# Reordering the hand-written schedule of a one-core infini-attention and MLP kernel: the same instructions, 234 and 235 changes of the matmul engine's tiling

## The chip, the cores and the metric

One core of a Trainium2 chip runs the kernel. The metric is the device time of one execution in microseconds (us). The engines are named as in the profile: PE is TensorE with its matmuls, PEld its weight loads, DVE is VectorE, ACT is ScalarE, POOL is GpSimd, SP is SyncE, whose queue (SPq) issues nearly all DMA transfers here.

## The reference, cut to what matters

The kernel adds an infini-attention and an MLP to its input x of 2048 tokens by 512 channels, in fp32:

```python
xn = _layernorm(x)
# attention: 32 heads of 16, 4 segments of 512 tokens; for each segment s
logits = einsum("bhqd,bhkd->bhqk", qs, ks) * scale + mask
p = softmax(logits);  a_dot = einsum("bhqk,bhkd->bhqd", p, vs)
pq = phi(qs);  a_mem = einsum("bhld,bhde->bhle", pq, M) / (einsum("bhld,bhd->bhl", pq, z)[..., None] + 1e-6)
o = g * a_mem + (1.0 - g) * a_dot
M = M + einsum("bhld,bhle->bhde", phi(ks), vs);  z = z + einsum("bhld->bhd", phi(ks))
# MLP: 512 -> 1792 -> 512
y = _layernorm(xn);  h = _gelu(y @ w1 + b1);  mlp = h @ w2 + b2
return x + o @ wo + mlp
```

## The kernel before

**Jobs and units.** The attention is cut into 16 units (4 segments by 4 groups of 8 heads), numbered 0 to 15. The work is a list of 1308 jobs, each a function that issues instructions to several engines. Jobs of one kind form streams (`streams()`), in which their order is fixed. `ORDER` is a string of 1308 letters: each letter names the stream whose next job is issued. `plan()` reads it, and the last loop of the kernel calls the jobs. The schedule is manual: every engine executes its own instructions in the order in which they were issued, and waits only for the semaphores of what it needs. So `ORDER` alone decides what stands behind what on PE, DVE, ACT, POOL and in SP's queue. `BANKS` gives, in the order of the calls, the PSUM bank (0 to 7) of each tile that `dense()` hands out.

**The jobs that matter here.**
- T(i,1), T(i,0) (`qk_proj`): keys and queries of unit i, 12 matmuls with 512 columns on the whole array (L495). ACT (L529) and DVE (L533) split the result into two fp16 halves, SP stores them to DRAM (L534 to L536) and loads them back in another layout into `kst` and `qst` (L542). For the memory, DVE forms phi in place (L544, L545).
- M(i,0) to M(i,11): row maxima of the logits. PE (L636) in two row halves of the array, DVE reduces (L643) into `mc`.
- R(i) (`m_row`): transposes `mc` (L514), splits the maxima (ACT L653, DVE L654), sends them through DRAM (SP L656, L659) into two more rows of `qst`. The scores S wait for it.
- S(i,t,n): logits minus maximum (PE L676 in row halves), exponential (ACT L681), triangle cut (POOL L690).
- pv and PV: probabilities times values (PE L705, in column tiles of 32); the second half is added by DVE (L718, L719).
- O(i,0) to O(i,2) (`o_norm`): normalises, adds the memory part and splits: DVE L729, ACT L555 and L556, DVE L560 and L561, POOL L735 and L737, ACT L740, POOL L741.
- Z, Qd, Q: the memory read (PE L586, ACT L591, DVE L592; Q: ACT L555 and L556, DVE L560 and L561, POOL L598).
- D(j,f): first MLP matmul, 12 matmuls with 256 columns on the whole array (L495 on `w1s`), DVE L771. G(j): gelu, with an ACT table load. H(j,c): split of the hidden values (POOL L785, ACT L786, POOL L787).
- e(j,n), n from 0 to 13: second MLP matmul, six matmuls in two row halves (L812). At n = 7 the halves exchange their PSUM banks, and `swap` makes PE wait until the earlier matmuls of that j have ended. DVE L818 adds the sum at n = 13.
- out(3,b): the output projection, 12 matmuls (L830), DVE L833 and the store L752. The four of the last segment end the program.
- X: loads and normalises 128 rows of x (SP L459).

PE thus works in three tilings: the whole array (T, D, V, out), two row halves (M, S, e, Qd and the transposes), and four column tiles (pv, PV, K).

Of the kernel before, what the change touches and what calls it, by code (L numbers as in the profile page):

```python
# [57 lines left out]
def streams():  # L58
# [43 lines left out]


ORDER = (
    "atacctcaetcttetcawvavcatwvcaxeacatxvdccwvxwfttyyyxbxyyuxgyyyzozoywouoxyccyzhoAzzAootAAppciiizAznpBiiABfBncAiBpi"
    "gzBszniipnzBiimchqqqiCBqBqiiioAoACBCCBCjjqiojqAjqjcioijoiCikskkBcmDskioBjiqiqCjjoijqCiqjsCqjDiftaoCCpgkkkpkjqCj"
    "oloojjljoloojiipkkkkiqihspqijqqipqijqiqjsjqqjaajfgpiiqkkkkmpliqqiooiqpDlqoDopohijjiojiijpolsjiqaqajqiqiqqiiqapk"
    "akmkktspaqijqiqjqiqajqbqajopijjgDfopkkkDkjjjlooooDlhjjjolqiqqiipkkkkjiqqijqqjjiqiqjjqiqiqiDkkkkmpliilfnplimpngr"
    "rmrjjponijqjqjinjipiskmkkmkaiijrijjoojiqsjqqjiqiiiqqkkkkihlqlfmlogojqjqjqqjjasoojmkkkkmqjiqjqjjaojjpipmooisikkk"
    "klpilhiofmgoooqiqpppqiqiqqqiiiqqpsosmoiqqiiqiqppsslooijqjojijojijoiaakkkkmpaijqjqjaqqqjiqqjiqjqiikmkkakbqiaqqah"  # L110
    "lolfqjjojqmjgjjoolmmkkkkmhjjoojjiitjiojiippkkkkliiilnfnimpligniinipmrrijjrsijqjqiqjiqjqiipkmkkksiqjqijqjqjiqjqi"
    "iqjqikmpkkkiprlqsphlfojmjgopjjlojpjoomokmkkkqiqisjojiqisjqiqijqqijqhiqqiiqjsqiiqppmkkkkilalofomqpgopaoooospmlaj"
    "qqqjqqjqjqiiqiqqqjqiqqipipooooiijooppoiaakkkkmajiqpisqqjiqjqjaiqaqhjqqqjqaaqmkkkkbjlfoljqjmjgojjqolmkkkkmmjjjoo"
    "jjioijoiiippkpkkkiinliifniiilnnimlgrpmjjrmjjjrrijikkpskkiqqijqiqijqqjiqjiqjqiqjiqiispqkpkskksqilqoplfojmjgjjjpo"
    "ooojolmkkkkiqjiqpsjiqiqijqjqiqijqjiqiqiqiiqqkksmkpikplolfjjqmjgjjjoooooklpkmkkjiiopjqiqijqjiqpjqiqijqiqqiqiiqik"
    "kpspkkqiplpoooopljjjqqqjqjjqooolkpskmkpkmqqqpqjpjqqqjqjqpqqjqjqqqkmkkkqlllqqqqqqqqqrrrr"
)

BANKS = (
    "050123614061756123401632157467410534702651305176254301741260523716405142730612547306651240651024615024612504612"
    "504650124650412650412650412650142650142650421607653420107642531076425031702531270531270531270132570132570132576"
    "135402761350427163054273106542736574326574326537425632754632574631072456310724563071245360712453620731620731067"
    "203617621073621073621073621037621037621037261702361475023671540263701524603175246031746013746013713460713471630"
    "471630463714067314056723410523674105236741052367410527410527410527410527410527140352671450326475103264751023674"
    "523674523647253647236547236475264735264107532410765324107265431067512043675120436751204736152047361520473615270"
    "346150312750317250317253107250371257013275027135027134650132754062751340621375460376054370567403056374065374065"
    "307645307645307642153076241076241076241076253410762534621075346210754316024310264310432610432610324610324612403"
    "246013752640163754207156437120564371205647312056473120564731206547321065473265104723607423460273460273642073642"  # L130
    "073642051736420157642031765420316750316705315631705630157630157630157306173504621357462017345620147536210436024"
    "136024316403216403216403216403216740536740536740536740536271406"
)


# [790 lines left out]
```

## Time and profile before

| | |
|---|---|
| device time, median of 3 | 691.06 us (690.85 to 691.38) |
| the profiled execution, device time | 691.51 us |
| span of its trace | 689.8 us |
| around the span | 1.7 us |
| mean granted TensorE clock | 0.999 of full speed |
| busy share PE / DVE / ACT / POOL | 99% / 79% / 73% / 49% |

The span runs from the first to the last instruction of the trace. A busy share is an average over the whole span. The rows below give the start of a group of like instructions, the time that it covers, and in brackets how long its engine was idle before it and what released it.

### The profile page before, as it was taken

To read this page: it belongs to the slowest core of one execution; us is meant where nothing else is said; L and a number is where in the kernel's file an instruction comes from. 1 tells how busy PE (TensorE), PEld (TensorE's weight loads), DVE (VectorE), ACT (ScalarE), POOL (GpSimd) and SP (SyncE) were. 2 spreads that over 40 slices of the span, in tenths; PEclk is the share of its full clock that TensorE was granted. 3 is DMA by queue.
4 is the path that set the end of the run, shared out by engine and by line. 5 is a ranking of instruction groups with operands and counts; after the bars stand their busy time and mean duration, and the time that the engine had idled before them with its cause. 6 is when DMAs were issued, how large, how long until landed. Compare 5 with 4: busy or idle time off the path is not lost.

```text
span 689.8 us, 17163 instructions
## 1 busy us (share of the span) xinstructions
PE 681.8 (99%) x6465; PEld 399.8 (58%) x6465; DVE 545.7 (79%) x1740; ACT 502.9 (73%) x972; POOL 340.5 (49%) x526
## 2 busy tenths in 40 slices
PE   8999999999999999999999999999999999999997
PEld 7855655565654546566554557567564456656653
DVE  6999968897795887998797787888688696969442
ACT  4486897788786659856794796766795687878870
POOL 5355567456535334663435355454353545446752
PEclk9999999999999999999999999999999999999999
DMA  9856342421203322421213224231120415140101
GB/s 277 249 149 201 92 109 49 117 55 31 65 24 102 94 67 45 122 50 33 69 26 98 58 73 100 72 86 32 41 72 24 132 19 154 17 109 2 19 1 62
DMA packets 51792, 55.15 MB, mean 80 GB/s; under 512 B 4782, under 2 KB 40636, under 8 KB 51708
## 3 DMA queue, kind: packets, MB, share of 16 engines
q1 hardware_dynamic: 49404, 49.84, 24.9%
q0 software_dynamic: 2304, 4.20, 3.8%
q8 instruction: 51, 0.84, 0.5%
q14 instruction: 33, 0.27, 0.1%
HBM read 36.99 MB, written 17.04 MB: 78 GB/s over the span
## 4 chain that ended last, share of the span: by engine, by line
PE 85%; DVE 5%; ACT 5%; DMA 2%; POOL 1%; issue 1%; SPq 0%; POOLq 0%; DVEq 0%; ACTq 0%
PE ps L495 36%; PE ps L812 17%; PE ps L705 10%; PE ps L830 6%; PE ps L676 5%; PE ps L636 5%; DVE ps L643 3%; ACT pt L681 2%; PE ps L586 2%; PE ps L514 1%; PE ps L843 1%; PE ps L321 1%; DMA wks<-in_A_wk_dram 1%; DMA qd<-hl 1%; PE ps L617 1%
## 5 line engine op out<-in xcount | busy, mean ns | idle before, releaser
L643 DVE CUSTOM_DVE_ANT_0 ps<-ps,mask 128x512 f32<-128x512 f32 (+3 forms) x512 | 233.9, 523 | 14.1 <-PE ps L636 12.9
L681 ACT ACTIVATE pt<-ps,qkcs 128x512 f32<-128x512 f32 (+1 forms) x384 | 206.8, 624 | 37.3 <-PE ps L676 35.2
L812 PE MATMUL ps<-w2s,hT 64*128 64x512 f16 x1344 | 176.6, 375 | 0.1
L495 PE MATMUL ps<-xnT,w1s 128*128 128x256 f16 x1344 | 158.0, 273 | 0.0
L690 POOL TENSOR_SCALAR_AFFINE_SELECT pt<-pt 128x256 f32<-128x256 f32 x256 | 101.0, 421 | 98.2 <-ACT pt L681 97.2
L495 PEld LDWEIGHTS <-w1s 128*128 128x128 f16 x1344 | 127.2, 98 | 28.5 <-issue 11.6
L787 POOL TENSOR_TENSOR hT<-hh,hT 128x512 f16<-128x512 f32 x64 | 67.7, 1057 | 86.3 <-ACT hT L786 82.7
L812 PEld LDWEIGHTS <-hT 64*128 64x128 f16 x1344 | 76.3, 94 | 49.8 <-issue 5.9
L705 PE MATMUL ps<-pt,vt 128*32 128x512 f32 (+3 forms) x1024 | 77.1, 435 | 0.1
L771 DVE SCALAR_TENSOR_TENSOR hT<-ps,sc,sr 128x256 f32<-128x256 f32 x112 | 52.4, 478 | 26.9 <-PE ps L495 26.7
L643 DVE DVE_READ_ACCUMULATOR2_ANT mc<- 128x1 f32 x512 | 71.0, 139 | 0.0
L636 PE MATMUL ps<-kst,qst 48*128 48x256 f16 (+3 forms) x512 | 66.7, 297 | 1.1 <-DMA qst<-qd 0.3
L676 PE MATMUL ps<-qst,kst 50*128 50x512 f16 (+3 forms) x512 | 66.2, 297 | 0.0
L786 ACT ACTIVATE hT<-hh 128x512 f16<-128x512 f32 x64 | 36.6, 572 | 33.3 <-POOL hh L785 32.9
L705 PEld LDWEIGHTS ps<-pt,vt 128*32 128x32 f32 x1024 | 30.5, 109 | 43.0 <-issue 32.4
L785 POOL TENSOR_SCALAR hh<-hT,sc 128x512 f32<-128x512 f32 x64 | 42.2, 660 | 25.7 <-ACT hT L778 24.1
L735 POOL TENSOR_TENSOR nN<-nN,oT 128x512 f32<-128x512 f32 x16 | 20.3, 1269 | 61.1 <-DVE oT L561 61.1
L778 ACT ACTIVATE hT<-hT,b1t 128x256 f32<-128x256 f32 x112 | 46.5, 495 | 0.2
L495 PE MATMUL ps<-xnT,wqs 128*128 128x512 f16 x192 | 44.2, 380 | 0.0
L495 PE MATMUL ps<-xnT,wks 128*128 128x512 f16 x192 | 44.1, 379 | 0.0
L495 PE MATMUL ps<-wvs,xnT 128*128 128x512 f16 x192 | 44.0, 379 | 0.0
L830 PE MATMUL ps<-wos,oT 128*128 128x512 f16 x192 | 43.3, 379 | 0.6 <-POOL oT L741 0.6
(225 smaller groups left out, 883.1 us busy)
## 6 DMA issues: line engine op xcount, KB each, us to landing
kd<-hl SPq DMA_DIRECT2D x48, 128.0 KB
qd<-hl SPq DMA_DIRECT2D x48, 128.0 KB
kst<-kd SPq DMA_DIRECT2D x32, 192.0 KB
qst<-qd SPq DMA_DIRECT2D x32, 192.0 KB
acc<-in_A_x_dram SPq DMA_DIRECT2D x16, 256.0 KB
acc<-in_B_b_dram POOLq DMA_DIRECT2D x16, 256.0 KB, 4.2
out_dram<-acc SPq DMA_DIRECT2D x16, 256.0 KB
xt<-in_A_x_dram SPq DMA_DIRECT2D x14, 256.0 KB
```

The lines of the kernel that those rows point to most:

```text
L495: T.matmul(p, wsl(ws, k, a), xsl(xs, k, b), start=s0 and i == 0, stop=s1 and i == 3 * n - 1)
L636: T.matmul(p[:, o:o + n], stk[i, 0][r, t, P * qb:P * qb + P], stk[i, 1][r, t, :n], start=True, stop=True)
L643: V.tensor_tensor_reduce(p[:, o:o + n], p[:, o:o + n], mask[:, 512 - n:], 1.0, -3e38, OP.add, OP.max, mc[:, 16 * b + 4 * t + qb:16 * b + 4 ...
L676: T.matmul(p[:, o:o + n], stk[i, 1][r, t, P * kb:P * kb + P], stk[i, 0][r, t, P * kb:], start=True, stop=True)
L681: A.activation(e[:, OFF[kbs[0]]:OFF[kbs[0]] + o], p[:, :o], AF.Exp, scale=qkcs[:, 1, i % NG:i % NG + 1])
L690: G.affine_select(v, v, pattern=[[0, 2], [1, P]], compare_op=OP.is_ge, fill=0.0, base=0, channel_multiplier=-1)
L705: T.matmul(p[32 * c:32 * c + 32, P * kb:], vt[s, kb][:, 4 * g + c, 16 * odd:16 * odd + 32], pt[i, 2 * c + odd][:, OFF[kb]:OFF[kb] + LEN[kb ...
L771: V.scalar_tensor_tensor(hz[:, fi, :], p[:, :256], col(F1 + fh), srow[hs][:, own], op0=OP.mult, op1=OP.mult)
L778: A.activation(z, z, AF.Gelu_apprx_tanh, bias=b1t[:, FH * (j % 2) + f:FH * (j % 2) + f + 1])
L787: G.tensor_tensor(hT[:, z, 1, :], t, hT[:, z, 0, :], op=OP.subtract)
L812: w = T.matmul(pes[j][a], hTs[fh][r, fi, u, P * a:P * a + P], w2s[r, fo, v, :], start=n == 0 and m == 0, stop=fi == FH - 1 and m == 2, ski ...
L830: T.matmul(p, o[:, u, P * b:P * b + P], wos[:, g, v, :], start=i == 0, stop=i == 3 * NG - 1)
```

## The change

Only the two tables `ORDER` and `BANKS` are replaced. The first 60 jobs are the same, and behind them the same jobs come in another order. Both kernels issue 1308 jobs and the same instructions (9859 rows on PE in each). PE changes between its three tilings 234 times in the order before and 235 times in the new one. The banks are handed out anew for the new order. The last line of `ORDER` shows the kind of change; all other lines behind the first half line differ in the same way.

```diff
 ORDER = (
...
-    "kpspkkqiplpoooopljjjqqqjqjjqooolkpskmkpkmqqqpqjpjqqqjqjqpqqjqjqqqkmkkkqlllqqqqqqqqqrrrr"
+    "iqikkkkoiplooopljjjqojqmjqqjolospkkkpkqmpqjpqqqqqqjqqjjqpqjqjmqqqkkkkqlqqqqlqqqlqqqrrrr"
 )
...
 BANKS = (
...
-    "136024316403216403216403216403216740536740536740536740536271406"
+    "714302743102743102740342317024317021473050763205376207356204207"
 )
```

In these lines k is a pv or PV job, q an e job, j an S job, l an O job, o a D job, m a memory job, p a G or H job, i an M or R job and r an out job.

SP's queue behind T(2,1) and T(2,0), the keys and queries of unit 2, before: the stores to `kd_93` and `qd_95` are theirs, L542 loads them back, and L459 loads rows of x for the next segment.

```order
L656 DMA md_98<-mhl 32x2x128
L659 DMA qst_90<-md_98 2x2048 x2
L534 DMA kd_93<-hl 8x16x512
L535 DMA kd_93<-hl 8x16x512
L536 DMA kd_93<-hl 8x16x512
L459 DMA xt<-in_A_x_dram 128x512 x2
L534 DMA qd_95<-hl 8x16x512
L535 DMA qd_95<-hl 8x16x512
L536 DMA qd_95<-hl 8x16x512
L542 DMA kst_91<-kd_93 48x4x512 x2
L542 DMA qst_89<-qd_95 48x4x512 x2
L791 DMA acc<-in_A_x_dram 128x512
```

The same place now:

```order
L534 DMA kd_93<-hl 8x16x512
L535 DMA kd_93<-hl 8x16x512
L536 DMA kd_93<-hl 8x16x512
L656 DMA md_98<-mhl 32x2x128
L659 DMA qst_90<-md_98 2x2048 x2
L534 DMA qd_95<-hl 8x16x512
L535 DMA qd_95<-hl 8x16x512
L536 DMA qd_95<-hl 8x16x512
L542 DMA kst_91<-kd_93 48x4x512 x2
L542 DMA qst_89<-qd_95 48x4x512 x2
L791 DMA acc<-in_A_x_dram 128x512
L459 DMA xt<-in_A_x_dram 128x512 x2
```

The x loads have moved from ahead of the query stores to behind the loads into `kst` and `qst`, and the trip of unit 1's maxima (L656, L659) from ahead of the key stores to behind them.

DVE around R(15), the maxima of the last unit, before: L718 and L719 belong to PV(14,1), L654 to R(15), L729 to O(14,0), L771 to the D(15) jobs.

```order
L718 SCALAR_TENSOR_TENSOR nN<-ps_9812,bg,nN 128x512
L719 SCALAR_TENSOR_TENSOR nD<-ps_9812,eo,nD 128x512
L654 SCALAR_TENSOR_TENSOR mhl<-ps_9851,mhl 32x64
L654 SCALAR_TENSOR_TENSOR mhl<-ps_9852,mhl 32x64
L729 STREAM_SHUFFLE oT<-nD 128x512
L771 SCALAR_TENSOR_TENSOR hT_116<-ps_9875,sc,sr 128x256
```

The same place now:

```order
L718 SCALAR_TENSOR_TENSOR nN<-ps_9829,bg,nN 128x512
L719 SCALAR_TENSOR_TENSOR nD<-ps_9829,eo,nD 128x512
L771 SCALAR_TENSOR_TENSOR hT_116<-ps_9848,sc,sr 128x256
L654 SCALAR_TENSOR_TENSOR mhl<-ps_9863,mhl 32x64
L654 SCALAR_TENSOR_TENSOR mhl<-ps_9864,mhl 32x64
L729 STREAM_SHUFFLE oT<-nD 128x512
```

D(15,0) has moved from behind R(15) to ahead of it, so that three D jobs instead of four are left between R(15) and the first scores S(15,0,0) that wait for it.

PE where e(14,6) ends and e(14,7) begins, before: `ps_9979` and `ps_9980` are the two sums of e(14), and the pair comes in the other order from e(14,7) on; L676 is S(15,1,0) and then S(15,1,1).

```order
L812 MATMUL ps_9979<-w2s,hT_115 128x512
L812 LDWEIGHTS hT_115
L812 MATMUL ps_9980<-w2s,hT_115 128x512
L676 LDWEIGHTS kst_92
L676 MATMUL ps_10148<-qst_90,kst_92 128x512
...
L676 MATMUL ps_10159<-qst_90,kst_92 128x128
L812 LDWEIGHTS hT_115
L812 MATMUL ps_9980<-w2s,hT_115 128x512
```

The same place now, with the sums `ps_10016` and `ps_10017`:

```order
L812 MATMUL ps_10016<-w2s,hT_115 128x512
L812 LDWEIGHTS hT_115
L812 MATMUL ps_10017<-w2s,hT_115 128x512
L812 LDWEIGHTS hT_115
L812 MATMUL ps_10017<-w2s,hT_115 128x512
```

The two score jobs that stood between the last matmul of e(14,6) and the first of e(14,7) have moved away, so that nothing is left between them.

At the end of the program, between PV(15,1) and out(3,0), there are 11 e jobs now and 10 before; between PV(14,1) and pv(15,0,0) 4 and 6; between PV(15,0) and pv(15,1,0) 15 and 16. There the order of the instructions on DVE, ACT and POOL is the same in both.

## Rows read from the trace of the kernel before

**Rows 1.** The page: busy time (share, instructions) of each engine; chain that ended last, by engine.

```profile
PE 681.8 (99%) x6465; PEld 399.8 (58%) x6465; DVE 545.7 (79%) x1740; ACT 502.9 (73%) x972; POOL 340.5 (49%) x526
PE 85%; DVE 5%; ACT 5%; DMA 2%; POOL 1%; issue 1%; SPq 0%; POOLq 0%; DVEq 0%; ACTq 0%
```

**Rows 2.** Timeline of PE at 300 us: start, length, instruction, count.

```profile
300.00 2.79 PE L495 MATMUL ps<-xnT,w1s 128*128 128x256 f16 x24
302.73 0.39 PE L636 MATMUL ps<-kst,qst 48*128 48x512 f16 x2
```

**Rows 3.** Windows: from:to, sum, busy of PE, PEld, DVE, ACT, POOL, clock, DMA, GB/s.

```profile
35.00:80.00 45.00, 44.25 (x411) 25.87 (x412) 43.35 (x161) 34.74 (x71) 24.43 (x33) 1.00 0.53 161
585.00:602.00 17.00, 16.81 (x187) 10.63 (x180) 16.84 (x73) 12.75 (x27) 7.51 (x14) 1.00 0.13 22
```

**Rows 4.** Timeline from T(2,0) to M(2,0): SP's queue and PE.

```profile
97.06 0.89 SPq L459 DMA_DIRECT2D xt<-in_A_x_dram  x2
...
104.66 0.79 SPq L542 DMA_DIRECT2D qst<-qd  x2
...
108.98 0.33 PEld L636 LDWEIGHTS <-qst 48*128 48x128 f16 x5 [0.36 <-DMA qst<-qd]
```

**Rows 5.** Timeline ahead of T(8,0).

```profile
332.61 1.26 POOL L737 TENSOR_TENSOR nN<-nN,ame 128x512 f32<-128x512 f32 x1
332.66 1.50 DVE L544 TENSOR_SCALAR phk<-phk,qksc 128x512 f32<-128x512 f32 x1
...
334.94 0.18 PEld L586 LDWEIGHTS ps<-phq,zr 64*128 64x128 f32 x1 [0.64 <-DVE phk L545]
```

**Rows 6.** All instructions of L544: count, shortest/median/longest in ns, first and last start.

```profile
L544 DVE TENSOR_SCALAR phk<-phk,qksc x12: 466/996/1503, 20.6 to 445.3; 128x512 f32<-128x512 f32 x12
L544 DVE TENSOR_SCALAR phq<-phq,qksc x12: 474/478/1396, 168.9 to 612.8; 128x512 f32<-128x512 f32 x12
```

**Rows 7.** Timeline from R(14) (601.14) to S(14,0,0) (605.69) and T(15,0) (608.19).

```profile
601.14 0.12 PEld L514 LDWEIGHTS ps<-ident,mc 64*96 64x96 f32 x2 [0.44 <-DVE mc L643]
...
601.33 0.43 PE L705 MATMUL ps<-pt,vt 128*32 128x128 f32 x8
...
605.69 0.61 PE L676 MATMUL ps<-qst,kst 50*128 50x512 f16 x6
...
607.65 0.61 PE L676 MATMUL ps<-qst,kst 50*128 50x256 f16 x2
...
608.19 0.60 PE L495 MATMUL ps<-xnT,wqs 128*128 128x512 f16 x2
```

**Rows 8.** Timeline from R(15) to S(15,0,0) (641.54), and S(15,2,0) (644.31).

```profile
636.01 0.25 PE L514 MATMUL ps<-ident,mc 64*96 64x64 f32 x2
...
636.20 5.41 PE L495 MATMUL ps<-xnT,w1s 128*128 128x256 f16 x48
...
641.54 0.91 PE L676 MATMUL ps<-qst,kst 50*128 50x512 f16 x8
...
644.31 0.65 PE L676 MATMUL ps<-qst,kst 50*128 50x512 f16 x2
```

**Rows 9.** Timeline of the last 25 us, from pv(15,1) to out(3,0).

```profile
665.01 0.15 PEld L705 LDWEIGHTS ps<-pt,vt 128*32 128x32 f32 x6 [0.42 <-POOL pt L690]
...
667.60 0.69 DVE L561 SCALAR_TENSOR_TENSOR rc<-rc,rt 128x512 f32<-128x512 f32 x1
...
667.73 6.89 PE L812 MATMUL ps<-w2s,hT 64*128 64x512 f16 x60
668.26 0.75 DVE L718 SCALAR_TENSOR_TENSOR nN<-ps,bg,nN 128x512 f32<-128x512 f32 x1
...
669.91 4.21 PEld L812 LDWEIGHTS <-hT 64*128 64x128 f16 x42 [0.56 <-PE ps L812]
...
674.55 2.67 PE L830 MATMUL ps<-wos,oT 128*128 128x512 f16 x11
...
677.85 8.16 PE L830 MATMUL ps<-wos,oT 128*128 128x512 f16 x37 [0.63 <-POOL oT L741]
```

More of the change, by code (lines that the diff above doesn't have):

```diff
@@ L104 @@
 ORDER = (
[L105 to L114, printed above, removed]
@@ L115 @@
-    "ooojolmkkkkiqjiqpsjiqiqijqjqiqijqjiqiqiqiiqqkksmkpikplolfjjqmjgjjjoooooklpkmkkjiiopjqiqijqjiqpjqiqijqiqqiqiiqik"
-    "kpspkkqiplpoooopljjjqqqjqjjqooolkpskmkpkmqqqpqjpjqqqjqjqpqqjqjqqqkmkkkqlllqqqqqqqqqrrrr"
+    "atacctcaetcttetcawvavcatwvcaxeacatxvdccwvxwfttyyyxbxyyuxgyyyzzuwyooooyzAoyAxzoozpiphizcntAcAccizipczBizfzBAniBi"
+    "BpgBCACniipiBnqiiqCqmhAqAiBiqBioBCCoBjAjojqiqjisqAsjqjisooiiCckmkBDBisikkoCjqijojiqjcCqiCqjjftiCCpogkkkkCjqpjlo"
+    "oojjljoloojipiskkkkihqapiqiqjipsqqjiqqjijqqijaqijfgomkiDqpapiqqqhiskkkpDlooiojlijoDojjiiopjiqaqaqipsjqiqlipitap"
@@ new lines @@
+    "kakkmkqqjqaiqqqjiqaqabiqjjopjjigpfokkkkjjloojjljpoooqjliqihkkkkiqiDqjiqjqmqjiqiDqqjqjjqiaqqikkkkDpliiinDlnflimp"
+    "grnjjsmjrrojsiijnjiikkskmkpijioripjjojiqqjqiiqjqipqikkkkhmiqlolfmjgojqqjqjjaqjlookkkmkmjiqjqqjjoijojmpiikkkapks"
+    "lhiopoolfimipgopopqiqqqqiqipqiimqqooiiqlqipioojiqjqjqjsiopojiiojasamakkpkmkijqqjqjaqsjqqqjiqiqjiakkisbkkhqiaqal"
+    "olfojqjqqjmjgjjoolkkkmkmjhjmoojjitijjoiiikpkkkpnliiilfniimgniiplniprrpjjirijqjqqjiiqqjiksmakkkmiqjqijsqjqijqiqj"
+    "qijpriikkkkhqiplqomlfmjjgopjolojjjookkkmkmiiqjqqppqiiojiqjsqiqjiqmjqhjpqiqqispikkkkliqqipoolsfoimpgooopmojjqqqa"
@@ L117 @@
+    "qjqqjqisjpqaiqqiipqiqiooqpiqljipooosooaaikkkkiqsqjaiqpqiqjjqqajaqijqqjqqaakkmmkkbjlolhjfjqmjgqjjolokmkkkmjjoojm"
+    "jijooiijkkkpiipinpkliiilfnlniiinmigrrpmjjjrjjrjsiikkkksiqiqjiqqpijqqjiqjiqqjjmqiqipqiikkkkqiplqolfjmjsgopoljmjo"
+    "ojmjoposkkkkiqjpsiqjiqiqjsiqqjiqiqjiqqijqiqiikskpkpkilolfqjjqmjgjpjjooookklmkkoijipojqijqijqpjiqqjiiqqpiqpqipqi"
+    "iqikkkkoiplooopljjjqojqmjqqjolospkkkpkqmpqjpqqqqqqjqqjjqpqjqjmqqqkkkkqlqqqqlqqqlqqqrrrr"
 )
 BANKS = (
-    "050123614061756123401632157467410534702651305176254301741260523716405142730612547306651240651024615024612504612"
@@ L123 @@
[L123 to L131, printed above, removed]
-    "136024316403216403216403216403216740536740536740536740536271406"
+    "050123614061756123401632157467032471456024371560247532610472653014657230614230576410576410574067156047156047516"
@@ new lines @@
+    "041075641075610765410761450764510741064571064571542603762154307462513407265406725620475276045276074256077406746"
+    "312056734014725630147253601427534127534127543125741325741325714352160741351264031752640317640253140245310425310"
+    "423103542103541270561342740651302174653242610754324610753624107562413507624135067241367241376234127613423761432"
+    "761432673142673142567017342056017345675426103746251403754103751401753403157043157043162745031672540364157023642"
+    "531642513642135643145623164152315642376012341520746351402765314632051764235042173652410736205364103271503624713"
@@ new lines @@
+    "205647132647132647312467312467312471632471632174637213406572061435720635147026351745021457021452704175204175204"
+    "175240137054236052130764521430521435021345042135042342714560327016453725643754623756243755624357624573624574362"
+    "750143762503174625753014267503124753012465174623051274360754123716057042316045723410623416023416023416023041623"
+    "104165302174265301472635021576432016423061402361423062143062143061243061234064057123403605637124305671320471320"
+    "714302743102743102740342317024317021473050763205376207356204207"
```

## The prediction, put on record before the run

> **What bounds the kernel now.** I read the page first: PE is busy for 99% of the span, and the chain that ended last lies on PE for 85% [rows 1]. No other engine is near that over the whole span. So the time is PE's own work plus what PE loses between instructions, and an order can change only the second part: the cost of changing the tiling, waits, and the end. I then followed PE along its timeline and noted each place where it, or its weight loads, stood still for another engine or a transfer. The windows say which engine is behind: from 35 to 80 us DVE works 43.35 of 45 us, and from 585 to 602 us 16.84 of 17 us, at full clock in both [rows 3]. Everywhere else DVE, ACT and POOL have slack, and only single late results reach PE.
>
> The sum is made against the profiled execution, 691.51 us, of which 689.8 are span. It lies 0.45 above the median of 691.06, so I subtract 0.45 at the end. The bound of what can be told from no change is 0.2%, here 1.4 us.
>
> **Changes of tiling: +0.1.** The pitch shows their price. Two D jobs take 302.73 - 300.00 = 2.73 us up to the next instruction in row halves [rows 2]; four D jobs, again with a change behind them, take 641.54 - 636.20 = 5.34 [rows 8]. The difference of 2.61 is two D jobs, so a D is 1.305 and one change about 0.1. 234 changes are some 23 us, and 235 are 0.1 more. An e is 0.65: 42 of its matmuls take 674.55 - 669.91 = 4.64 us with a change behind them [rows 9], 0.108 each, and it has six.
>
> **The head, 35 to 80 us: -0.3.** Every job of the weight scaling, the first T, M and D comes in a new order there, but DVE has the same work. Only its idle 45 - 43.35 = 1.65 us can be gained [rows 3], and PE can be held longer if DVE's results come in a worse order. I take -0.3, with -1.0 (most of the idle time) and +0.7 (as much again as less than half of it) as bounds.
>
> **T(2,0) to M(2,0): -0.3.** M(2,0) waits 0.36 for `qst` [rows 4]. Its stores stood in SP's queue behind the x loads at 97.06, whose issue took 0.89, and the load L542 came at 104.66. Now the x loads stand behind. PE has the same six D, six S and one e to do in between. Bounds: 0 (ACT's half comes late in any case) and -0.36. What moves behind, the x loads, is wanted only by the next segment.
>
> **T(8,0): -0.5.** DVE's L544 took 1.50 us at 332.66, beside POOL's L737, which had begun 0.05 earlier and ran to 333.87 [rows 5]. A free L544 takes 0.47 [rows 6]. Behind it L545 came late, and the weights of Qd(7) waited 0.64 for DVE [rows 5]. Between T(8,1) and Qd(7) PE now has three e instead of two beside the same D and three S, 0.65 more to do, which covers it. Bounds 0 and -0.64.
>
> The Trainium skill bears on this, page "SBUF — State Buffer", section "Who interferes with whom": an operation of DVE in a two-port mode, which tensor_scalar can enter, and one of POOL take a shared port pair in turn, and the loser blocks until the other's whole instruction has ended. The trace agrees: 1.50 is nearly the 1.21 that L737 still had to run plus the free 0.47. By the row alone the term stands at -0.5; by the rule the gain can be lost again wherever the new order puts another L544 behind a POOL operation, which is the second rival.
>
> **M(14) and R(14): +0.4 and +0.2.** From 585 to 602 us DVE is full with the row maxima of M(14), and R(14) already waits 0.44 for `mc` [rows 3, 7]. The order before gives PE 13 e jobs between M(14,0) and R(14); the new one gives it 12 and PV(13,1), which is 0.43 at most [rows 7] against 0.65. PE has less to do in the same DVE time: 0.2 to 0.4 more waiting; bounds 0 and +0.7. Behind R(14) on DVE, L718 and L719 of PV(13,1) now stand ahead of L654 where L575 stood: two operations of 0.75 each [rows 9] for four small ones of some 0.2, so the maxima leave about 0.7 later. The trip from R to S was 605.69 - 601.14 = 4.55 without a wait [rows 7]; PE now has a D (1.3), T(15,1) (two D in columns, 2.6), an e (0.65) and changes, about 4.8. Some 0.2 may be waited for S(14,0,0), between 0 and 0.7.
>
> **T(15,0): -0.3.** S(14,0,2) at 607.65 and T(15,0) at 608.19 are 0.54 apart [rows 7], where a pair of S (0.108 a matmul at most, as in e) and a change need some 0.3. ACT is late with T(15,1) behind it. e(12,12) now stands between T(15,1) and S(14,0,0), which gives ACT 0.65 more. Bounds 0 and -0.3.
>
> **R(15) to S(15,0,0): +0.5.** Here PE had four D behind R, and S came 641.54 - 636.01 = 5.53 us after R without a wait [rows 8]. Now three D stand there, 4.0 to 4.2 us. The trip of the maxima through DRAM needs what the other units show: at most 4.55 in unit 14 [rows 7], at most 5.53 here. If it needs 4.3 PE waits 0.2; if it needs 5.0, 0.9. I take 0.5. SP and DVE have nothing new in the trip; L771 of D(15,0) goes ahead of L654, but its matmuls end before R's.
>
> **S(15,2,0): -0.2.** The pair of S(15,2,0) took 0.65 [rows 8] where a pair of that form takes 0.39 [rows 2]; its two banks are given free by ACT and by DVE's L818. With other banks that wait of 0.26 goes, or another comes: -0.26 to +0.3.
>
> **Swap: +0.2.** e(15,7) begins behind e(15,6) with nothing in between, and its weights wait 0.56 for PE to run empty [rows 9]. The 18 matmuls ahead of it end at 667.73 + 18 x 0.108 = 669.67, and the next begin at 669.91, so the emptying costs 0.24. In the order before this happens once in the tail; S(15,1,0) and S(15,1,1) hide it for e(14,7). In the new order nothing stands there: once more, 0 to +0.24.
>
> **The tail: -1.4.** This is the largest term. Before, pv(15,1) waits for POOL's triangle cut, 0.42 at first [rows 9]. L718 then cannot start when PV(15,1) is done, because DVE is at Q(15)'s L560 and L561 until 668.29; it starts at 668.26. From there the chain of O(15) (DVE, ACT, DVE, POOL, ACT, POOL) is serial and ends some 9.5 us later, when out(3,0), whose twelfth matmul needs it, goes on at 677.85. PE has done ten e and 11 matmuls of out(3,0) by 674.55 + 11 x 0.217 = 676.94 (512 columns cost twice a D matmul's 1.305 / 12) and waits 0.91 (0.63 at the matmul, the rest in its weight load). In the new order 11 e stand behind PV(15,1): 0.65 of the 0.91 is covered. PV(15,1) itself comes later against DVE and POOL, since 16 instead of 15 e stand ahead of pv(15,1,0) and Q(15) has been issued three e earlier: the 0.4 of the cut goes, and so does the 0.5 that L718 was held. Together 0.91 + 0.45, all of the waiting. At worst only 0.65 and part of the cut go, -0.9; at best -1.6. The work that PE does there is only shifted, and the last 37 matmuls and the store behind them stay as they are.
>
> **The sum.** 0.1 - 0.3 - 0.3 - 0.5 + 0.4 + 0.2 - 0.3 + 0.5 - 0.2 + 0.2 - 1.4 = -1.6, so 689.9 for the profiled execution, less 0.45: 689.4.
>
> **Rivals.**
> - The tail is gained and the rest gives it back: R(14), M(14) and R(15) at their upper bounds (0.7 + 0.7 + 0.9 in place of 1.1) and no gain in the head and at T(8,0) (0.8). That is -1.6 + 1.2 + 0.8 = +0.4, 691.5; with half of it, 690.5. For it speaks that distances behind most R are shorter now; against it that PE had slack in those trips.
> - Slower: L544 meets POOL elsewhere. There are 24 of them, 466 to 1503 ns, half of those on keys at 996 or more [rows 6], each up to 1.03 late, and PE pays for one of them now. It decides where PE's next need follows at once, at Qd or T. At four more paid in full, and the gain at T(8,0) gone, -1.6 + 4.1 + 0.5 = +3.0: 694.1; from three on it is 693.1, slower by more than can be told from no change. Against it: most late L544 cost PE nothing in the order before.
> - More than I take: the head gives its whole idle time and T(2,0), T(8,0) and the tail their bounds, while M(14) and R(15) cost nothing: -1.6 - 0.7 - 0.2 - 0.2 - 1.1 = -3.8, 687.3.
> - Nothing happens: other waits appear at the tail, for example Q(15) ahead of the last S on ACT, and the order is worth 0.1: 691.1.
>
> **How the numbers follow.** My sum holds with 0.45 (688.5 to 690.2), the give-back with 0.25, more than I take with 0.12, nothing with 0.08, slower with 0.10. Faster by over 0.2%, below 689.7: two thirds of the first and all of the third, with a little of the second, 0.46; slower 0.11; the rest 0.43. The range goes from 687.6 to 691.6: it leaves out the far end of the third and the slower cases. The likeliest case's own range is 688.5 to 690.2.
>
> **What would show it.** In the new profile: PE's busy time within 0.5 us of 681.8; no [POOL] release at pv(15,1) and out(3,0) going on without a wait behind O(15); no wait for `qst` ahead of M(2,0); S(15,0,0) with a wait for a transfer behind three D; the pair e(14,6), e(14,7) with a weight load that waits for PE; DVE as full as before from 35 to 80 us. The prediction is wrong if out(3,0) still waits for POOL, if new releases by DVE or DMA at Qd, T or S sum to over 1.5 us, or if the head moves by more than 1 us.

## The result, and the profile after

The new order is slower. Its median over 6 runs is 694.43 us (693.08 to 695.44), against 691.10 us (690.44 to 691.52) for the order before in 6 runs beside it: a ratio of 1.0043, 95% interval 1.0031 to 1.0055, so 2.1 to 3.8 us longer. The forecast was 689.4 us with a range to 691.6. The profiled execution took 694.2 us, of which 692.5 are span; the clock was full in both.

The page of the new order, with the two lines that answer to [rows 1]:

```profile
PE 681.8 (98%) x6465; PEld 392.6 (57%) x6465; DVE 542.2 (78%) x1740; ACT 504.3 (73%) x972; POOL 341.6 (49%) x526
PE 80%; DVE 10%; DMA 5%; ACT 2%; issue 2%; SPq 0%; POOL 0%; DVEq 0%; POOLq 0%; ACTq 0%
```

PE's busy time is the same to a tenth, so the 2.7 us of span are all time between PE's instructions. The shares of DVE and DMA in the chain that ended last have doubled or more. To find the places I took, for sets of jobs that both orders have issued in full, the start of the next job on PE:

| jobs done | next job | before | after | after - before |
|---|---|---|---|---|
| 365 | T(4,1) | 166.88 | 165.90 | -0.98 |
| 539 | a D job | 266.91 | 265.97 | -0.94 |
| 659 | an e job, now a transpose | 323.90 | 324.22 | +0.32 |
| 731 | R(8) | 373.62 | 372.54 | -1.08 |
| 933 | K, now M | 479.17 | 480.20 | +1.03 |
| 993 | S(11,1,0) | 508.27 | 509.56 | +1.29 |
| 1086 | pv(12,1,1) | 563.64 | 565.29 | +1.65 |
| 1241 | e(13,12), now D(15,4) | 642.19 | 646.22 | +4.03 |
| | out(3,0) | 674.55 | 677.93 | +3.38 |
| | end of the span | 689.8 | 692.5 | +2.7 |

The new order leads by a microsecond at 166 and at 373 us. It loses 1.3 from 266 to 322 us, 2.1 from 373 to 479 us and 2.4 from 564 to 646 us. The list of PE's waits names a transfer for the largest (line waited at, what was waited for: us in total, times, longest):

```profile
PE ps L676 <- DMA qst<-md: 2.1, 2, 1.6
PE ps L636 <- DMA qst<-qd: 0.7, 1, 0.7
PE ps L514 <- DVE mc L643: 0.7, 2, 0.5
```

The 1.6 is at R(15). The timeline there, which answers to [rows 8]:

```profile
638.82 0.26 PE L514 MATMUL ps<-ident,mc 64*96 64x64 f32 x2
639.01 4.10 PE L495 MATMUL ps<-xnT,w1s 128*128 128x256 f16 x36
...
639.93 0.30 SPq L656 DMA_DIRECT2D md<-mhl  x1
...
643.07 0.54 SPq L659 DMA_DIRECT2D qst<-md  x2
...
644.75 0.73 PE L676 MATMUL ps<-qst,kst 50*128 50x512 f16 x6 [1.64 <-DMA qst<-md]
```

The maxima go to DRAM with L656 and come back with L659, which SP issues when the store has landed. From L656 to L659, here called the trip, it took 643.07 - 639.93 = 3.14 us. In the trace before it took 1.39 to 1.49 in ten of the 16 trips and 1.77 to 2.66 in the other six, 2.02 at R(15); now it takes 1.39 to 1.45 in nine and 2.31 to 3.18 in seven. R(15) before:

```profile
637.49 0.30 SPq L656 DMA_DIRECT2D md<-mhl  x1
...
639.51 0.53 SPq L659 DMA_DIRECT2D qst<-md  x2
```

In the new order the three D jobs behind R(15) last 4.10 us; R to S took 5.93. The DMA view from 639.9 to 643.1 us (queue: packets, MB, share of 16 engines' time) shows what else was under way:

```profile
q1 hardware_dynamic: 80, 0.02, 2.6%
q8 instruction: 1, 0.02, 2.4%
```

q1 carries the store, 80 packets; q8 is of the kind instruction, so what it moves is code, and one 16 KB piece of it is moved here, from 640.79 to 642.03. Where nothing else moves, the packets of the store pass in 0.2 us. Here the windows from 640.7 to 641 us (first two lines) and from 642 to 642.2 us (last line) show 75 of them beside the piece and the last five only when it has passed:

```profile
q8 instruction: 1, 0.02, 25.9%
q1 hardware_dynamic: 75, 0.02, 23.0%
q1 hardware_dynamic: 5, 0.00, 6.9%
```

The last packet ends at 642.17, and L659 follows 0.90 us later. Before, a piece of code (637.51 to 638.47) met the store of R(15) too, at the cost of 0.6 us that the four D jobs covered.

The second place is M(11,0), which waits for its queries:

```profile
448.21 0.33 SPq L656 DMA_DIRECT2D md<-mhl  x1
451.21 0.56 SPq L659 DMA_DIRECT2D qst<-md  x2
451.87 0.58 SPq L534 DMA_DIRECT2D qd<-hl  x1
...
456.79 0.79 SPq L542 DMA_DIRECT2D qst<-qd  x2
...
461.12 0.39 PE L636 MATMUL ps<-kst,qst 48*128 48x512 f16 x1 [0.72 <-DMA qst<-qd]
```

Here R(10)'s trip stands in SP's queue ahead of the query stores of T(11,0), and it too lasted 3.00 us (451.21 - 448.21), with a piece of code in it (449.15 to 450.10). In the order before those stores began at 449.16 and L542 came at 454.16, 2.6 earlier.

The third stretch shows no large wait, but a full DVE; in the timeline single waits for it, and the window from 290 to 300 us (columns as in [rows 3]):

```profile
283.99 2.78 PE L495 MATMUL ps<-xnT,w1s 128*128 128x256 f16 x24 [0.23 <-DVE phk L545]
298.97 2.78 PE L495 MATMUL ps<-xnT,w1s 128*128 128x256 f16 x24 [0.16 <-DVE mc L643]
301.91 0.39 PE L676 MATMUL ps<-qst,kst 50*128 50x512 f16 x2 [0.16 <-DVE mc L643]
290.00:300.00 10.00, 9.84 (x94) 6.33 (x91) 9.96 (x42) 4.81 (x10) 3.86 (x4) 1.00 0.41 89
```

Before, PE worked all of these 10 us and DVE 9.53. The waits of PE for DVE from 266 to 322 us, with one of 0.20 at 272.45, sum to 0.75; there were none before.

What answers to [rows 4] to [rows 7], at T(2,0), ahead of T(8,0) and at R(14):

```profile
102.90 0.79 SPq L542 DMA_DIRECT2D qst<-qd  x2
104.23 0.90 SPq L459 DMA_DIRECT2D xt<-in_A_x_dram  x2
108.01 0.43 PEld L636 LDWEIGHTS <-qst 48*128 48x128 f16 x6
...
332.40 0.48 DVE L544 TENSOR_SCALAR phk<-phk,qksc 128x512 f32<-128x512 f32 x1
332.57 1.44 POOL L737 TENSOR_TENSOR nN<-nN,ame 128x512 f32<-128x512 f32 x1
334.19 0.30 PEld L586 LDWEIGHTS ps<-phq,zr 64*128 64x128 f32 x4
...
602.57 0.26 PE L514 MATMUL ps<-ident,mc 64*96 64x64 f32 x2 [0.49 <-DVE mc L643]
```

M(2,0) and Qd(7) no longer wait, as forecast; R(14) still does, and longer: its weight load stood for 0.76 where it stood for 0.44 before. In the tail, which answers to [rows 9], POOL's two waits are still there, 0.42 at pv(15,1) and 0.52 at out(3,0), and e(14,7) now waits 0.56 for PE to run empty:

```profile
660.45 0.98 PEld L812 LDWEIGHTS <-hT 64*128 64x128 f16 x12 [0.56 <-PE ps L812]
668.04 0.28 PEld L705 LDWEIGHTS ps<-pt,vt 128*32 128x32 f32 x8 [0.42 <-POOL pt L690]
670.46 7.54 PE L812 MATMUL ps<-w2s,hT 64*128 64x512 f16 x66
677.93 10.74 PE L830 MATMUL ps<-wos,oT 128*128 128x512 f16 x48
680.50 7.67 PEld L830 LDWEIGHTS <-oT 128*128 128x128 f16 x37 [0.52 <-POOL oT L741]
```

### The profile page after: what moved, and what is told of

Its sections match the earlier page's. It is cut to its first block, busy times and chain, and to the rows that moved or that the text cites. A ratio compares the mean times of both kernels' runs of the same rounds, so it can differ in the third digit from the quotient of the medians.

```text
span 692.5 us, 17151 instructions
## 1 busy us (share of the span) xinstructions
PE 681.8 (98%) x6465; PEld 392.6 (57%) x6465; DVE 542.2 (78%) x1740; ACT 504.3 (73%) x972; POOL 341.6 (49%) x526
## 4 chain that ended last, share of the span: by engine, by line
PE 80%; DVE 10%; DMA 5%; ACT 2%; issue 2%; SPq 0%; POOL 0%; DVEq 0%; POOLq 0%; ACTq 0%
PE ps L495 34%; PE ps L812 17%; PE ps L705 9%; PE ps L830 5%; PE ps L676 5%; DVE ps L643 5%; PE ps L636 4%; DMA qd<-hl 2%; PE ps L586 1%; DMA qst<-qd 1%; DVE mc L643 1%; PE ps L514 1%; DMA md<-mhl 1%; ACT pt L681 1%; PE ps L321 1%
## 5 line engine op out<-in xcount | busy, mean ns | idle before, releaser
L681 ACT ACTIVATE pt<-ps,qkcs 128x512 f32<-128x512 f32 (+1 forms) x384 | 207.3, 620 | 43.2 <-PE ps L676 41.7
L812 PE MATMUL ps<-w2s,hT 64*128 64x512 f16 x1344 | 174.1, 376 | 0.1
L690 POOL TENSOR_SCALAR_AFFINE_SELECT pt<-pt 128x256 f32<-128x256 f32 x256 | 102.6, 427 | 94.6 <-ACT pt L681 93.9
L812 PEld LDWEIGHTS <-hT 64*128 64x128 f16 x1344 | 70.0, 94 | 56.6 <-issue 4.2
L771 DVE SCALAR_TENSOR_TENSOR hT<-ps,sc,sr 128x256 f32<-128x256 f32 x112 | 51.6, 477 | 24.1 <-PE ps L495 22.1
L676 PE MATMUL ps<-qst,kst 50*128 50x512 f16 (+3 forms) x512 | 64.7, 298 | 2.2 <-DMA qst<-md 2.1
L705 PEld LDWEIGHTS ps<-pt,vt 128*32 128x32 f32 x1024 | 31.9, 109 | 40.2 <-issue 30.3
L676 PEld LDWEIGHTS <-kst 50*128 50x128 f16 x512 | 26.2, 94 | 31.7 <-issue 12.1
```

Of the source, the lines that this page charges most:

```text
L676: T.matmul(p[:, o:o + n], stk[i, 1][r, t, P * kb:P * kb + P], stk[i, 0][r, t, P * kb:], start=True, stop=True)
L681: A.activation(e[:, OFF[kbs[0]]:OFF[kbs[0]] + o], p[:, :o], AF.Exp, scale=qkcs[:, 1, i % NG:i % NG + 1])
L690: G.affine_select(v, v, pattern=[[0, 2], [1, P]], compare_op=OP.is_ge, fill=0.0, base=0, channel_multiplier=-1)
L705: T.matmul(p[32 * c:32 * c + 32, P * kb:], vt[s, kb][:, 4 * g + c, 16 * odd:16 * odd + 32], pt[i, 2 * c + odd][:, OFF[kb]:OFF[kb] + LEN[kb ...
L771: V.scalar_tensor_tensor(hz[:, fi, :], p[:, :256], col(F1 + fh), srow[hs][:, own], op0=OP.mult, op1=OP.mult)
L812: w = T.matmul(pes[j][a], hTs[fh][r, fi, u, P * a:P * a + P], w2s[r, fo, v, :], start=n == 0 and m == 0, stop=fi == FH - 1 and m == 2, ski ...
```

## The experiments

Each ratio is to the order before, run on the same chip, with its 95% interval. In the diffs `before` and `after` stand for the two orders of 1308 letters; where pieces are joined, both have issued the same jobs up to the joint. The banks are fitted to each joined order.

### How much R(15) costs: one D job moved back, and the same move in the order before

a_r15: the new order with four D jobs behind R(15); e(13,11) takes the place of D(15,0).

```diff
 ORDER = (
...
-    "iqikkkkoiplooopljjjqojqmjqqjolospkkkpkqmpqjpqqqqqqjqqjjqpqjqjmqqqkkkkqlqqqqlqqqlqqqrrrr"
+    "iqikkkkqiploooopljjjojqmjqqjolospkkkpkqmpqjpqqqqqqjqqjjqpqjqjmqqqkkkkqlqqqqlqqqlqqqrrrr"
```

> The new order with one place put back: e(13,11) ahead of R(15) and D(15,0) behind it, so that four D jobs instead of three cover the trip of the last unit's maxima through DRAM; all else as in the new order. Theory 'trip': the 1.64 us that PE stood at S(15,0,0) goes, 1.0 to 1.7 us faster than the new order, so about 692.7 to 693.4. Rival 'collisions spread out' (DVE and POOL meeting at many places): no single place matters, within 0.5 us of the new order's 694.4.

b_r15: the order before with three D jobs behind R(15).

```diff
 ORDER = (
...
-    "kpspkkqiplpoooopljjjqqqjqjjqooolkpskmkpkmqqqpqjpjqqqjqjqpqqjqjqqqkmkkkqlllqqqqqqqqqrrrr"
+    "kpspkkoiplpooopljjjqqqqjqjjqooolkpskmkpkmqqqpqjpjqqqjqjqpqqjqjqqqkmkkkqlllqqqqqqqqqrrrr"
```

> The order before with only that place changed as the new order has it: D(15,0) ahead of R(15), e(13,11) behind S(15,0,2). Theory 'trip': S(15,0,0) waits for the maxima, 0.2 us if the store of the maxima lands in 1.4 us, up to 1.7 if a transfer of code meets it; 691.3 to 692.8, and a wider spread of the times. Rival: the order before has the slack anyway, within 0.2 of 691.1.

Measured: a_r15 1.0024 (1.0014 to 1.0035), b_r15 1.0017 (1.0008 to 1.0027). The move is worth about 1.3 us in the new order (1.0043 - 1.0024, give or take 1.1) and costs 1.2 (0.6 to 1.9) in the order before. So this one step explains less than half of the loss, but it was more than twice my +0.5. In a_r15 the trip still lasted 3.12 us from store to load and PE still waited 0.6 behind four D: the trip itself is what is long. In the trace of b_r15 PE waits only 0.30 at S(15,0,0), behind a trip of 1.92, so most of its 1.2 us is not seen at that place.

### Is it the code transfer: PE's program shifted by a few instructions

after2 is the new order once more, beside the others. a_warm48 has the new order, but three of the 14 warm-up jobs at the start do their 2048 columns in 16 matmuls of 128 columns instead of 8 of 256: the same PE time and 48 more instructions on PE (each matmul has a weight load), so that every later instruction stands 48 places further on. a_warm96 does it in six warm-ups. b_warm48 is the order before with the edit of a_warm48.

```diff
-        for _ in range(8):
-            T.matmul(p[:, :256], w[:, :P], w, start=True, stop=True)
+        c = 128 if n < 3 else 256
+        for _ in range(2048 // c):
+            T.matmul(p[:, :c], w[:, :P], w[:, :c], start=True, stop=True)
```

> The new order unchanged, once more, for comparison with the next kernel on the same chip: 1.0043 of the order before (1.0031 to 1.0055), as at first. At R(15) the code transfer of 16 KB lies over the store of the maxima again, the load is issued 2.5 to 3.2 us behind the store, and S(15,0,0) waits 1 us or more.

> The new order unchanged, but three warm-up jobs at the start have 16 matmuls of 128 columns instead of 8 of 256 (a result nobody reads): 48 more instructions in PE's program, the same columns. PE's code is fetched in pieces of 16 KB at fixed places of its program, so every fetch now comes 48 instructions earlier against the jobs, some 2.6 us among D jobs. Theory 'code fetch': at R(15) the fetch is over before the store of the maxima, the load is issued 1.4 us behind the store, S(15,0,0) waits 0 to 0.2 us instead of 1.6, and the kernel is 1.0 to 2.0 us faster than the new order. Rival (the three D are too short for the trip whatever else moves): the same wait, within 0.4 us of the new order.

> The new order with 96 extra instructions, in six warm-up jobs: the fetch comes some 5 us earlier against the D jobs than in the new order, and again off the trip of R(15). Theory 'code fetch': the load at R(15) is issued 1.4 us behind the store, no wait at S(15,0,0), 1.5 to 3 us faster than the new order, unless a fetch now meets another trip. Rival (only 48 is lucky): as slow as the new order.

> The order before with the same 48 extra instructions in the first three warm-up jobs. Theory 'code fetch on a short trip': the order before covers its trips (5.5 us of D jobs behind R(15)), so where the fetch falls is worth little: within 0.7 us (0.1%) of the order before. Rival ('the 48 instructions help by themselves', by PE's start or its warm-up): about 3 us faster here too.

Measured: after2 1.0042 (1.0030 to 1.0055); a_warm48 0.9997 (0.9989 to 1.0006); a_warm96 1.0009 (0.9999 to 1.0018); b_warm48 1.0004 (0.9994 to 1.0014). Behind the warm-up only the place of PE's instructions in its code has changed, and the new order gets faster by 3.1 us with 48 instructions and 2.3 with 96; the order before does not. after2 repeats what was seen at first: trips of 2.90 at R(15) and 3.38 at R(10), each with a piece of code in it, and waits of 1.48 and 0.60 behind them. R(15) in a_warm48:

```profile
638.41 0.26 PE L514 MATMUL ps<-ident,mc 64*96 64x64 f32 x2
638.61 4.11 PE L495 MATMUL ps<-xnT,w1s 128*128 128x256 f16 x36
...
639.52 0.30 SPq L656 DMA_DIRECT2D md<-mhl  x1
...
640.92 0.53 SPq L659 DMA_DIRECT2D qst<-md  x2
...
642.65 0.92 PE L676 MATMUL ps<-qst,kst 50*128 50x512 f16 x8
```

and its DMA view from 639.5 to 641 us, which has no q8:

```profile
q1 hardware_dynamic: 80, 0.02, 4.9%
```

The piece of code came at 637.26 here, 2.3 us ahead of L656. The same three D jobs, the same queue, and L659 follows after 1.40 us, 0.36 behind the last packet. Only a weight load still waits, 0.22. The trip of R(10) is also short again:

```profile
448.39 0.33 SPq L656 DMA_DIRECT2D md<-mhl  x1
449.86 0.57 SPq L659 DMA_DIRECT2D qst<-md  x2
...
454.69 0.79 SPq L542 DMA_DIRECT2D qst<-qd  x2
...
460.07 0.38 PE L636 MATMUL ps<-kst,qst 48*128 48x512 f16 x2
```

A load of ACT's tables, the other thing that falls into this trip, is no rival: it lies there in both traces, 0.75 us behind L656 in the new order (640.68 to 641.96) and 0.80 in a_warm48 (640.32 to 641.60). The packets of all 18 traces say the same of their 288 trips. The 133 with no other transfer between L656 and L659 took 1.38 to 1.46 us, 57 of them beside a table load. The 30 whose store met a piece of code on q8, and nothing else, took 1.92 to 3.32; 18 with an 8 KB piece on q14, the other queue of the kind instruction, 1.68 to 2.53; 59 with only other data of the kernel, 1.39 to 3.28.

The lag that was +1.29 at S(11,1,0) is 508.63 - 508.27 = +0.36, and the +4.03 at 1241 jobs is 644.15 - 642.19 = +1.96. a_warm96 also has a 1.40 trip at R(15); its trace has other waits, 1.22 at the first scores for one: a shift moves the collisions, it does not abolish them. The order before does not care, since four D cover its trip even at 2.02 us (1.39 in b_warm48), and b_warm48 rules out that 48 instructions help by themselves.

The Trainium skill, page "Runtime: NRT & Kernel Launch", section "Instruction fetch mechanics", says that each engine's instruction memory is refilled in pieces of 16 KiB, 256 instructions, by a DMA queue that its sequencer drives, and that crossing such a boundary is mostly hidden. The trace agrees on the pieces (51 transfers of 16 KB on q8 before, 50 after). Where a short store stood in its way such a transfer was not hidden here: it cost 1.64 us of waiting at one place, and moving the pieces was worth 3.1 us over the program.

### Where the rest is: pieces of the new order in the order before

Three pieces of the new order alone, the head alone, and one order that does not depend on the joints: a_r10 is the whole new order with R(10) ahead of T(11,1). (D(10,2) did not move with it, otherwise than its expectation says: it still stands behind T(11,1).)

```diff
-ORDER = before
+ORDER = before[:539] + after[539:659] + before[659:]     # b_539_659, 266 to 322 us
+ORDER = before[:659] + after[659:731] + before[731:]     # b_659_731, 322 to 371 us
+ORDER = before[:731] + after[731:933] + before[933:]     # b_731_933, 371 to 479 us
+ORDER = after[:539] + before[539:]                       # b_head, to 266 us
```

```diff
 ORDER = (
...
-    "qijpriikkkkhqiplqomlfmjjgopjolojjjookkkmkmiiqjqqppqiiojiqjsqiqjiqmjqhjpqiqqispikkkkliqqipoolsfoimpgooopmojjqqqa"
+    "qijpriikkkkhqiplqomlfmjjgopjolojjjookkkmkmiiqjqqppqiiojiqjsqiqjiqmjqhjpqiqqispikkkkliqqipoolsifompgooopmojjqqqa"
```

> The order before with one piece of the new order, from 266 to 322 us (the maxima of unit 6 and 7). Theory 'places': +1.2 us, since DVE is full there and PE waits for it in small steps at D(6,5), M(6,11), D(7,2), S(6,0,0). Rival: no change (0.2).

> The order before with one piece of the new order, from 322 to 371 us (T(8,1), T(8,0), the jobs of unit 7's scores). Theory 'places': -1.2 us, what PE's lag in the new order loses there. Rival: the lag shrinks there only because it grew just ahead of it, no change (0.2).

> The order before with one piece of the new order, from 371 to 479 us, with R(10) between T(11,1) and T(11,0). Theory 'queue': the stores of unit 11's queries stand behind the trip of R(10) in SP's queue, M(11,0) and M(11,1) wait 0.9 for them, and S(8,0,0) 0.3 to 0.5 for its own trip: +1.2 to +2.0 us. Rival: the new order's lag grew there for what came ahead of the piece, no change (0.3).

> The new order up to S(5,3,0) at 266 us, the order before from there (the same 539 jobs are done at the cut). Prediction: -0.6 from the head and T(2,0); the traces of both orders: -0.8 at the cut. So 0.6 to 0.9 us faster than the order before. Rival: the gain is given back behind the cut, within 0.3.

> The new order with R(10) and D(10,2) moved ahead of T(11,1), so that in SP's queue the maxima's store and load stand ahead of the key stores of unit 11 and no longer between its key and its query stores. Theory 'queue': the load waits for the store's landing and held the query stores for 3 us, so M(11,0) comes without its 0.9 us of waiting: 0.6 to 1.0 faster than the new order, 693.4 to 693.8. Rival: the stores are late because T(11,0) is, no change (694.2 to 694.6).

Measured: b_539_659 1.0016 (1.0007 to 1.0025), as expected: this piece costs 1.1 us by itself, and its trace goes from +0.81 to +2.06 across it and keeps that to the end (+2.00). b_659_731 0.9991 (0.9982 to 1.0000): a gain of 0.6, half of what I expected; its trace leads by 0.98 at 371 us, by only 0.26 at 479, and is 1.1 behind at the end. b_731_933 1.0003 (0.9994 to 1.0012): a miss, no loss to be seen in time where I had expected 1.2 to 2.0 us; its trace, of the slowest of its 11 runs, does lose 1.0 across the piece, but M(11,0) does not wait, and R(10)'s trip took 1.46 from store to load, with no code in it. b_head 1.0008 (0.9997 to 1.0019): a miss; the lead of 0.88 at 92 us is still 0.6 at 563 us and 0.3 at the end. In between the trips of R(14) and R(15) took 2.36 and 2.65 instead of 1.40 and 2.02; the store of the first met an 8 KB piece on q14, that of the second a piece on q8, and PE waited 0.37 and 0.19 behind them. a_r10 1.0084 (1.0069 to 1.0098): a miss by far. The wait for a transfer at M(11,0) went and R(10)'s trip took 1.41, but PE came to R(10) before DVE had the maxima, and the kernel lost 2.8 us against the new order, about half of it in one wait of 1.46 at R(10):

```profile
PE ps L514 <- DVE mc L643: 2.1, 3, 1.5
```

Much of this fits costs that hang on which transfers meet a trip, but with one trace for each piece it is not shown place by place. The piece from 266 to 322 us is another matter: it loses by itself, and the waits that can be seen there are for DVE (0.60 in b_539_659).

### The tail alone

b_tail is the order before up to S(15,0,2) and the new tail behind it; b_tail2 has e(13,12) and e(13,13) elsewhere in it.

```diff
 ORDER = (
...
-    "kpspkkqiplpoooopljjjqqqjqjjqooolkpskmkpkmqqqpqjpjqqqjqjqpqqjqjqqqkmkkkqlllqqqqqqqqqrrrr"
+    "kpspkkqiplpoooopljjjojqmjqqjolospkkkpkqmpqjpqqqqqqjqqjjqpqjqjmqqqkkkkqlqqqqlqqqlqqqrrrr"
```

> The order before up to S(15,0,2), and from there the new order (the same 1241 jobs are done at that cut in both): the new tail alone, with the four D behind R(15). Theory of the prediction: -1.4 us (-0.9 to -1.6), 689.7. Rival: the tail's gain is taken back by its own new waits, 690.8 to 691.3.

```diff
-    "kpspkkqiplpoooopljjjojqmjqqjolospkkkpkqmpqjpqqqqqqjqqjjqpqjqjmqqqkkkkqlqqqqlqqqlqqqrrrr"
+    "kpspkkqiplpoooopljjjqojqmjqjolospkkkpkqmpqjpqqqqqqjqqjjqpqjqjmqqqkkkkqlqqqqlqqqlqqqrrrr"
```

> The first run of the tail, with e(13,12) put ahead of D(15,4) and e(13,13) behind S(15,2,0), so that D(15,4) no longer waits for a bank behind ACT's exponentials (0.7 to 0.9 us there). Theory 'tail': -1.0 to -1.4 us against the order before. Rival: within 0.4 of it.

Measured: b_tail 1.0001 (0.9990 to 1.0012), b_tail2 1.0003 (0.9994 to 1.0012), both against the 1.4 us that this tail was to bring. b_tail waited 0.7 at D(15,4) for a bank that ACT's L681 still read; b_tail2 was to cure that and did not:

```profile
646.08 0.82 PE L812 MATMUL ps<-w2s,hT 64*128 64x512 f16 x6 [0.38 <-ACT pt L681]
647.24 2.78 PE L495 MATMUL ps<-xnT,w1s 128*128 128x256 f16 x24 [0.22 <-ACT pt L681]
...
677.70 6.37 PEld L830 LDWEIGHTS <-oT 128*128 128x128 f16 x31 [0.58 <-POOL oT L741]
```

The wait at the end is smaller (0.58 in a weight load, for 0.91 in all before), but it is not gone, and as much is lost behind S(15,0,2) on banks that ACT has not freed and in the second emptying of PE.

### Putting together what gains

mix2 takes the new order's pieces that led in the trace, and the old ones elsewhere; mix2_warm48 adds the shift of 48 instructions; a_m6_warm48 is the shifted new order with the old piece from 266 to 322 us.

```diff
-ORDER = before
+ORDER = after[:539] + before[539:659] + after[659:731] + before[731:1241] + tail     # mix2
+ORDER = after[:539] + before[539:659] + after[659:]                                  # a_m6_warm48
```

Here `tail` is that of b_tail with e(13,12) ahead of D(15,4) and e(13,13) behind S(15,2,0).

> Pieces of both orders, cut where the same jobs are done: the new order up to 266 us, the order before from 266 to 322 us, the new one from 322 to 371 us, the order before from 371 us to the scores S(15,0,2), then the new tail with e(13,12) ahead of D(15,4) and e(13,13) behind S(15,2,0) so that D(15,4) need not wait for a bank. Theory 'places' (each piece keeps what the traces show for it): -0.85 at the head, -1.2 from T(8,0), -1.0 to -1.3 in the tail, none of the new waits: 3 us below the order before. Rival (gains and losses move with the rest of the order): within 1 us of the order before.

> The version of pieces (mix2) with the 48 extra instructions. In mix2 the fetch lay over the trip of R(15) and PE waited 0.5 us behind four D. Theory: that goes, 0.3 to 0.8 us faster than mix2, 0.997 to 0.9975 of the order before. Rival: no change against mix2 (0.9982).

> The new order with the 48 extra instructions, and the piece from 266 to 322 us (the maxima of units 6 and 7) taken from the order before. Theory: the loss of 1.1 us that this piece showed in the order before is the same here, 0.998 to 0.9985 of the order before, against 0.9997 without. Rival: with the fetch out of the way the piece costs nothing, 0.9997.

Measured: mix2 0.9982 (0.9973 to 0.9991), 690.75 us against 692.54; mix2_warm48 0.9967 (0.9953 to 0.9981), 689.84 against 692.02; a_m6_warm48 0.9977 (0.9969 to 0.9986). All three beat both orders. a_m6_warm48 against a_warm48 gives the piece from 266 to 322 us a second time: 0.9997 - 0.9977 is 1.4 us, give or take 0.9, beside 1.1 from b_539_659. The intervals of mix2 and mix2_warm48 overlap, so what the shift adds there is open; in the trace of mix2_warm48 a piece of code still met the trip of R(15), which took 1.98 for 2.86 in mix2.

## Why the prediction was wrong

The step that failed is "R(15) to S(15,0,0): +0.5", in its sentence "If it needs 4.3 PE waits 0.2; if it needs 5.0, 0.9". I took the length of the trip through DRAM as something that the other units show, and "SP and DVE have nothing new in the trip". It has no such length: with a piece of code moved at the same moment the step from store to load took 3.14 us instead of 1.40, and R to S needed 5.93 instead of 4.3 to 5.0. With the piece out of the way it needed 4.24 (642.65 - 638.41 in a_warm48), which is the low case of that sentence. The term measured 1.64 us in the trace, above its bound of 0.9, and about 1.3 in time. The same cause sits at M(11,0), where I had no term at all: 0.9 of the lag at S(11,1,0) that a_warm48 took back. It is not in every execution: in the trace of a_r15, the same program up to R(15), M(11,0) does not wait, at a trip of 2.81. The shift of 48 instructions is worth 3.1 us, as much as the 3.0 that were lost; the two traces show 2.1 of it. That moving PE's instructions takes the loss away is shown by the shift, and that the trips get short with it by the traces. Which engine a piece of q8 was for, the profile does not say; that it was PE's is inferred from the counts in the last section.

With the shift the order stood at -0.2 us (a_warm48), still not at -1.6. There the tail's **-1.4** failed, "Together 0.91 + 0.45, all of the waiting": alone it is worth 0 within 0.8 us. I followed only the chain of O(15), and not who frees the banks of the jobs behind S(15,0,2); my last rival had said that other waits could appear there. In the whole new order the lag does shrink by 1.3 from 1241 jobs to the end, in a_warm48 too, but that is an order that comes late into the tail; where the tail begins on time (b_tail2: -0.10 there and -0.15 at the end) nothing comes back.

The other terms:
- Head, -0.3: the lead of 0.8 to 1.0 us is there in the trace, with DVE busy 44.12 of 45 us from 35 to 80 us. In time it was not to be seen (b_head +0.6, from -0.2 to +1.3).
- T(2,0), -0.3: right, no wait for `qst` is left.
- T(8,0), -0.5: right in mechanism, the wait of 0.64 is gone; in time its whole piece brought 0.6 (0 to 1.2). L544 began 0.17 ahead of L737 and took 0.48, and this time L737 took 1.44 instead of 1.26. The Trainium skill's rule (page "SBUF — State Buffer", section "Who interferes with whom") is that, where both want the shared ports, who is second waits for the whole of the first; the trace agrees in direction, but L737 took 0.18 longer where 0.31 of L544 were still to run. The sum in the prediction was loose in the same way: 1.21 + 0.47 is 1.68, and L544 had taken 1.50. The rival built on the rule did not come: the median of the key form of L544 fell from 996 to 478 ns.
- M(14), +0.4, and R(14), +0.2: the weight load of R(14) waits 0.32 longer, and M(14,0) to S(14,0,0), with the same work on PE in it, takes 607.43 - 587.51 = 19.92 us for 605.69 - 586.12 = 19.57, so the first is right; S(14,0,0) did not wait, so the second is not.
- Swap, +0.2: right, the second emptying of PE is there, at 660.45, 0.56 in its weight load and 0.23 between its matmuls.
- T(15,0), -0.3, S(15,2,0), -0.2, and tilings, +0.1: too small to be told apart in what was run.
- Missed: the piece from 266 to 322 us, +1.1 to +1.4. I had said that outside two windows all engines have slack; from 290 to 300 us DVE was already busy for 9.53 of 10, and now is for 9.96, with single waits of some 0.2 on PE.
- Missed too: S(8,0,0) waits 0.43 at 378.52 behind R(8), whose trip of 3.18 had no code in it but some 0.39 MB of the kernel's own transfers.

The slower outcome had its 0.11, but by another mechanism than the one written there. What stays open: how the 1.1 to 1.4 us from 266 to 322 us split over the single waits, and how much of a_warm48's gain beyond R(15) and M(11) comes from other trips.

## What to carry to other kernels

Where a result makes a round trip through DRAM, do not take its shortest observed time as its length: list the times of all trips in a trace, and give the longest of them as cover in the work behind it, or expect the order to win or lose by which transfers, pieces of code and its own data, happen to meet it. Before an order is judged, time it with PE's program shifted by a few dozen instructions: here the same order was 0.4% slower or equal by that alone. And a gain read off one engine's last wait, as in the tail, is only as good as the next wait behind it, so look at who frees the banks there.

## What the runs showed of the hardware that was not expected

A single 16 KB transfer of code, about 1.2 us long, delayed the landing of a 16 KB store that otherwise passes in 0.2 us. The store's packets began 0.06 us ahead of it; 75 of the 80 passed beside it, and the last five came when it was over, the last 0.14 us behind it. A load of ACT's tables in the same trip did not delay it (1.38 to 1.46 us from store to load in 57 trips).

And the piece comes at nearly the same count of PE's instructions each time. In 17 of the 18 traces, of both orders, of mixed ones and of the shifted ones, the 16 KB pieces between 595 and 645 us start when PE has begun 11,458 to 11,490, 11,694 to 11,710, 11,946 to 11,986 and 12,192 to 12,203 recorded instructions, matmuls and weight loads, whatever the time; in mix2_warm48 they come at 11,453, 11,715, 11,968 and 12,235. They are some 243 recorded instructions apart, near the 256 that a piece holds by the Trainium skill (the same page and section); some records are missing from every trace. With 0, 48 and 96 more instructions on PE the last of these pieces keeps to PE's count (12,202, 12,194 and 12,203) and not to DVE's (1,964, 1,954 and 1,945). So the collision at R(15) came in each execution of that code that was traced (trips of 3.14, 2.90 in after2, 3.12 in a_r15), and is moved by instructions that are added on PE in front of it.
